# Another order of the same instructions: priorities disturbed from a recorded list of 82 seeds in place of the best of 105 candidates

## The chip, the cores and the metric

The kernel runs on one core of a Trainium2 chip. A core has TensorE (PE, with its weight loads shown apart as PEld), VectorE (DVE), ScalarE (ACT), GpSimd (POOL) and SyncE (SP), which here issues every DMA. The metric is the device time of one execution in microseconds; the kernel is given by the median of its runs.

## The reference

x is 2048 tokens of 512 features. The result is x + s * g. s is a linear attention block on the normalised x with 32 heads of 16 features, g is the silu of a gated feed-forward block on the raw x with 1792 hidden features:

```python
def _A_ref(x, wqkv, wo):                       # H = 32, Dh = 16
    ...
    phi = lambda t: jnp.where(t > 0, t + 1, jnp.exp(t)) + 1e-6
    pq, pk = phi(q), phi(k)
    kv = jnp.einsum("bhsd,bhse->bhde", pk, v)
    z = jnp.einsum("bhsd->bhd", pk)
    num = jnp.einsum("bhqd,bhde->bhqe", pq, kv)
    den = jnp.einsum("bhqd,bhd->bhq", pq, z)[..., None] + 1e-6
    o = num / den
    return (...) @ wo

def _B_ref(x, w_gate, w_up, w_down):
    return (_gelu(x @ w_gate) * (x @ w_up)) @ w_down

x = A_x
xn = _layernorm(x, axis=-1)
s = _A_ref(xn, A_wqkv, A_wo)
g = _silu(_B_ref(xn, B_w_gate, B_w_up, B_w_down))
return x + s * g
```

## The kernel before, in words

Each large matrix product is done by a scheme with seven block products in place of eight (numbered 1 to 7 in the code), and each factor is split into a high and a low part (names that end in h and l), so that a product is three matmuls per block of 128 rows, a group of six for two blocks. One 512-column matmul is the unit of work on PE.

The program has four stages. In the first, x is loaded tile by tile, normalised and transposed (tiles x, xn, pt), its transposed forms Xh and Xl are made, keys and queries are computed (X, Y, Z, k, q) and the products of keys and x are summed up in four banks (gps). The queries and the forms of x for the first half go out to DRAM. In the second and third stage the feed-forward block is computed for the second half of the tokens and then for the first: quads of products FX, FY, FZ for one block of the gate or up weights, whose result h is split into seven forms hf0 to hf6 with a high and a low part, and down products DX, DY, DZ, which VectorE adds to acc. In the second stage the weights are taken from the inputs, brought into their forms and kept in DRAM (w_d, wd_d); the third stage loads them from there (w<-w_d, wd<-wd_d) and, between its quads, fetches the queries (q<-q_d), divides them (GpSimd makes u, VectorE den and q) and transposes them (ptq). Between these stages stand the small products of the attention block (pkv, pm), and the forms of x for the first half are loaded back (Xh<-xh_d, Xl<-xl_d). The last stage multiplies the queries with the folded attention weights (SX, SY, SZ), multiplies the result with the silu of the feed-forward block (g, acc), transposes it (rt), adds x (xp) and stores it (out_y).

No instruction is issued while the stages are described. Each call of do() only notes an operation: its engine, its planned duration (for example pool(n) is 0.15 + 0.00214 * n us), its dependences, and for a DMA its size. At the end Plan.order() makes one list of all operations, and they are issued in that list's order; every engine runs its own in the order of the list and waits on semaphores. So the list fixes each engine's queue, SP's DMA issues included.

Plan.run() is a list scheduler: an engine that is free takes, of the operations that are ready, the one with the lowest value in late. With the argument chain it also keeps to the stated order of the PE operations, pe_keys; with wide it does not. link() sets the lag between dependent operations, with three margins: to PE, to the other engines, and on the landing of a DMA. Plan.replay() goes through a finished list with the planned durations and gives start times and a total. A run backwards (with self.behind) turns start times into new values of late.

Before, order() did this for three sets of margins with 35 rounds each, noted for every round the total of a replay without margins, and gave back the list with the lowest one; where the best of a set of margins had not improved for more than two rounds, late was disturbed at random for all operations at once:

```python
if best is None or true < best[0] - 1e-6:
    best = true, done, at
...
if same > 2:
    size = rng.choice((0.05, 0.2, 0.5))
    late = [t + rng.uniform(-size, size) for t in late]
```

Of the kernel before, what the change touches and what calls it, by code (L numbers as in the profile page):

```python
# [75 lines left out]
class Plan:  # L76
# [6 lines left out]
    SLOW, FULL = 1.3, 6.0  # L83
    WAY = 0.45
    BEGIN = 0.65
    ROUNDS = 35
    MARGINS = ((0.1, 0.18, 1.0), (0.2, 0.06, 1.0), (0.1, 0.12, 1.0))
    SEED = 2
    WAIT = 0.3
    FIXED = 4  # L90

# [96 lines left out]
    def run(self, nxt, late):  # L188
# [75 lines left out]
        return start, done  # L264

    def replay(self, order):

        info = self.info
        ready, start = [self.BEGIN] * len(order), [0.0] * len(order)
        left = [len(row) for row in self.behind]  # L270
        queue = {e: collections.deque() for e in self.TAIL}
# [5 lines left out]
        while n < len(order):  # L277
            turn = None
            for e, q in queue.items():
                if q and not left[q[0]]:  # L280
                    t = max(free[e], ready[q[0]])
                    t = (max(t, port) if info[q[0]][2] else t, t, e)
                    if turn is None or t < turn:
                        turn = t
            when, _, eng = turn
            pick = queue[eng].popleft()
            n += 1
            _, cost, lock, move = info[pick]
            start[pick] = when
            end = free[eng] = when + cost  # L290
            if lock:
                port = end
            if eng == "SP":
                dma = max(dma, end + self.WAY)
                dma += move * (self.SLOW if dma < self.FULL else 1.0)
                end = dma
            last = max(last, end)
            for j, lag in self.ahead[pick]:
                if end + lag > ready[j]:
                    ready[j] = end + lag  # L300
                left[j] -= 1
        return last, start

    def order(self, pe_keys):
        self.link(pe_keys, 0.0, 0.0, 0.0)
        plain = self.ahead
        best, rng = None, random.Random(self.SEED)
        for margins in self.MARGINS:
            chain = self.link(pe_keys, *margins)
            wide = self.ahead  # L310
            late = self.tails(chain)
            low = min(late)
            late = [t - low for t in late]
            top, same = None, 0
            for n in range(self.ROUNDS):
                start, done = self.run(chain if n < self.FIXED else wide, late)
                total, real = self.replay(done)
                self.ahead = plain
                true, at = self.replay(done)
                self.ahead = wide  # L320
                if best is None or true < best[0] - 1e-6:
                    best = true, done, at
                if top is None or true < top[0] - 1e-6:
                    top = true, total, done, real
                    same = 0
                same += 1
                if same > 2:
                    _, total, done, real = top
                back = self.behind
                if n < self.FIXED - 1:  # L330
                    back = [[] for _ in chain]
                    for i, row in enumerate(chain):
                        for j, lag in row:
                            back[j].append((i, lag))
                start, _ = self.run(back, [total - t - c[1] for t, c in zip(real, self.info)])
                late = [total - t - c[1] for t, c in zip(start, self.info)]
                if same > 2:
                    size = rng.choice((0.05, 0.2, 0.5))
                    late = [t + rng.uniform(-size, size) for t in late]
            self.log(best[0])  # L340
        self.at = {self.ops[i]: t for i, t in enumerate(best[2])}
        return [self.ops[i] for i in best[1]]

    def log(self, total):
        pass
# [1077 lines left out]
```

## Time and profile before

| | |
|---|---|
| median of 3 runs | 612.13 us (610.62, 612.13, 614.85) |
| profiled execution, its own time | 610.86 us |
| its span, first to last instruction | 609.1 us |
| instructions | 8384 |
| PE busy | 601.8 us, 2754 matmuls |
| VectorE, GpSimd, ScalarE busy | 479.7, 359.9, 336.2 us |
| DMA | 143.16 MB, 67.2% of 16 engines' span in the main queue |

All rows come from one profiled execution, whose time lies between the lowest run and the median. The span leaves out what lies before the first and after the last instruction of the program, 1.7 us. A busy share says how long an engine had an instruction in work; matmuls overlap, since one is shown from its start to its modelled end and the next begins before that.

### The profile page before, as it was taken

Reading aid. Unit: us, or ns where it says so; the run is one execution under the profiler, and the core shown is the slowest. Engines: PE = TensorE matmul, PEld = TensorE weight load, DVE = VectorE, ACT = ScalarE, POOL = GpSimd, SP = SyncE. Lnnn points to the kernel's source line nnn. Section 1 sums busy time; section 2 is a strip of 40 time slices with the busy share of each in tenths; the row PEclk is TensorE's granted clock in tenths of the full one; section 3 lists DMA queues with packets and bytes.
Section 4 is the critical chain, followed back from the end, with each engine's and each line's share of the span. In section 5 each row is a group of like instructions: output and inputs, shape, how many; then the busy total and the mean of one; then the engine's idle time right before and its main releaser. Section 6 shows DMA issues by size and latency. Waiting matters only on the chain.

```text
span 609.1 us, 8384 instructions
## 1 busy us (share of the span) xinstructions
PE 601.8 (99%) x2754; PEld 496.2 (81%) x2754; DVE 479.7 (79%) x712; ACT 336.2 (55%) x610; POOL 359.9 (59%) x300
## 2 busy tenths in 40 slices
PE   9999999999999999999999999999999999999996
PEld 8888888888888888888888788888888888878884
DVE  6999988785887998788878556677837875879886
ACT  6787778785676635653564154545224522677520
POOL 5834644544879768967785047267306641686970
PEclk9999999999999999999999999999999999999999
DMA  7369521249768648864669799898558855996346
GB/s 241 101 217 305 190 69 71 86 156 343 278 210 291 225 151 312 314 210 170 210 241 404 297 350 414 317 290 270 159 204 273 291 168 189 331 337 217 119 162 218
DMA packets 69659, 143.16 MB, mean 235 GB/s; under 512 B 5616, under 2 KB 28144, under 8 KB 69616
## 3 DMA queue, kind: packets, MB, share of 16 engines
q1 hardware_dynamic: 69616, 142.63, 67.2%
q8 instruction: 22, 0.36, 0.3%
q14 instruction: 21, 0.17, 0.1%
HBM read 81.00 MB, written 61.60 MB: 234 GB/s over the span
## 4 chain that ended last, share of the span: by engine, by line
PE 96%; DVE 1%; DMA 1%; POOL 0%; issue 0%; ACT 0%; DVEq 0%
PE FX L496 24%; PE DX L496 13%; PE FZ L496 12%; PE gps L496 7%; PE DZ L496 6%; PE FY L496 6%; PE X L496 5%; PE SX L496 4%; PE DY L496 3%; PE Z L496 3%; PE k L496 2%; PE SZ L496 2%; PE q L496 2%; PE Y L496 1%; PE pt L666 1%; PE ptq L1148 1%
## 5 line engine op out<-in xcount | busy, mean ns | idle before, releaser
L496 PE MATMUL FX<-Xh,w 128*128 128x512 f32 x448 | 152.5, 390 | 0.0
L1056 POOL TENSOR_TENSOR h<-h,g 128x512 f32<-128x512 f32 x42 | 62.9, 1500 | 96.4 <-DVE h L480 95.0
L496 PEld LDWEIGHTS FX<-Xh,w 128*128 128x128 f32 x448 | 83.8, 188 | 17.2
L480 POOL TENSOR_TENSOR h<-h,h 128x512 f32<-128x512 f32 x56 | 84.5, 1508 | 12.9 <-DVE hf6l L480 4.1
L496 PE MATMUL FX<-Xl,w 128*128 128x512 f32 x224 | 87.4, 390 | 0.0
L496 PE MATMUL FZ<-Xh,w 128*128 128x512 f32 x224 | 78.5, 391 | 0.0
L474 ACT COPY fu<-FX 128x512 f32<-128x512 f32 x56 | 32.9, 587 | 66.9 <-PE FX L496 65.0
L496 PE MATMUL gps<-pks,xns 128*128 128x512 f32 x192 | 51.0, 391 | 0.0
L496 PEld LDWEIGHTS FX<-Xl,w 128*128 128x128 f32 x224 | 42.1, 188 | 8.7
L496 PEld LDWEIGHTS FZ<-Xh,w 128*128 128x128 f32 x224 | 41.7, 188 | 9.0 <-DVE g L480 0.6
L742 POOL TENSOR_TENSOR zacc<-zacc,kp 128x512 f32<-128x512 f32 x16 | 24.2, 1511 | 37.0 <-DVE kp L731 31.0
L496 PE MATMUL FZ<-Xl,w 128*128 128x512 f32 x112 | 43.9, 392 | 0.0
L1082 DVE TENSOR_TENSOR acc<-acc,DX 128x512 f32<-128x512 f32 x48 | 32.6, 682 | 14.3 <-PE DX L496 13.9
L496 PEld LDWEIGHTS gps<-pks,xns 128*128 128x128 f32 x192 | 35.9, 188 | 7.4
L496 PE MATMUL FY<-Xh,w 128*128 128x512 f32 x112 | 39.5, 394 | 0.0
L480 DVE TENSOR_TENSOR g<-fu,FZ 128x512 f32<-128x512 f32 x28 | 19.2, 685 | 17.0 <-PE FZ L496 7.7
L1082 DVE TENSOR_TENSOR acc<-acc,DZ 128x512 f32<-128x512 f32 x32 | 21.9, 683 | 12.7 <-PE DZ L496 9.0
L496 PE MATMUL X<-kq,Xh 128*128 128x512 f32 x96 | 31.1, 397 | 0.0
L1048 ACT ACTIVATE g<-g 128x512 f32<-128x512 f32 x42 | 26.6, 632 | 7.9 <-DVE g L480 7.8
L480 DVE TENSOR_TENSOR h<-fu,FZ 128x512 f32<-128x512 f32 x28 | 19.2, 685 | 14.3 <-PE FZ L496 7.6
L480 POOL TENSOR_TENSOR u<-q,zacc 128x512 f32<-128x512 f32 x16 | 21.0, 1331 | 11.9 <-DMA q<-q_d 11.3
L496 PEld LDWEIGHTS FY<-Xh,w 128*128 128x128 f32 x112 | 21.0, 188 | 4.7 <-issue 0.5
(413 smaller groups left out, 1621.3 us busy)
## 6 DMA issues: line engine op xcount, KB each, us to landing
w_d<-w SPq DMA_DIRECT2D x36, 512.0 KB, 5.1
w<-w_d SPq DMA_DIRECT2D x36, 512.0 KB, 5.1
wd_d<-wd SPq DMA_DIRECT2D x21, 512.0 KB, 4.9
wd<-wd_d SPq DMA_DIRECT2D x21, 512.0 KB, 5.6
x<-in_A_x SPq DMA_DIRECT2D x16, 256.0 KB, 4.0
q_d<-qp SPq DMA_DIRECT2D x16, 256.0 KB, 2.2
q<-q_d SPq DMA_DIRECT2D x16, 256.0 KB, 5.2
pn_d<-pT SPq DMA_DIRECT2D x8, 512.0 KB, 6.4
```

Source lines behind the costliest of these rows:

```text
L474: do("ACT", act(n), lambda o, i: nc.scalar.copy(o, i), dst, src, name=name)
L480: do(eng, c, lambda o, p, q: getattr(e, f"tensor_{op}")(o, p, q), dst, a, b, name=name)
L496: nc.tensor.matmul(o, v[i], v[i + 1], start=start and part == 0 and i == 0, stop=stop and part == 1 and i == len(v) - 2, skip_group_check=on)
L666: nc.tensor.transpose(o[:, k, :], a[:, k * P:(k + 1) * P], b)
L742: do("POOL", pool(D), lambda o, i: nc.gpsimd.tensor_add(o, o, i), zacc, p0, name="zacc")
L1048: curved("gelu", do("ACT", curve(NC), lambda o, i: nc.scalar.activation(o, i, AF.Gelu_apprx_tanh), g, ps if e is None else g, name="gelu"))
L1056: do("POOL", pool(NC), lambda o, i: nc.gpsimd.tensor_mul(o, o, i), h, g, name="h")
L1082: do("DVE", dve(NC), lambda o, i: nc.vector.tensor_add(o, o, i), a, ps, name="acc")
L1148: nc.tensor.transpose(o[:, k, :], a[:, k * P:(k + 1) * P], b)
```

## The change

The operations, their planned durations and their dependences stay as they are. order() first makes one list: 14 rounds with the margins (0.1, 0.12, 1.0), the first four with the stated order of PE and the others without, no random part, no comparison of rounds. Then it goes through a list of 82 seeds. For each, nudged() draws an instant of the plan, a width of 4, 10 or 25 us before it, a size of 0.2, 0.6 or 2.0 us and a share of 0.1, 0.4 or 1.0, and adds a random amount of up to that size to late for that share of the operations which the last plan started between that width before the instant and 2 us after it. Plan.run() then schedules all operations anew. The disturbed priorities are kept from seed to seed, and the list after the last seed is the one issued. The search that picked the seeds (by the mean of eight replays with longer operations and landings) is not part of the kernel.

```diff
@@ -83,9 +83,9 @@
     SLOW, FULL = 1.3, 6.0
     WAY = 0.45
     BEGIN = 0.65
-    ROUNDS = 35
-    MARGINS = ((0.1, 0.18, 1.0), (0.2, 0.06, 1.0), (0.1, 0.12, 1.0))
-    SEED = 2
+    ROUNDS = 14
+    MARGIN = (0.1, 0.12, 1.0)
+    STEPS = (4, 5, 15, 18, 44, 51, 56, 57, 89, 96, 99, 103, ...)
     WAIT = 0.3
     FIXED = 4
 
@@ -301,45 +301,55 @@
                 left[j] -= 1
         return last, start
 
+    def plan_times(self, done):
+
+        keep, self.ahead = self.ahead, self.plain
+        _, at = self.replay(done)
+        self.ahead = keep
+        return at
+
+    def first_order(self, pe_keys):
+
+        self.link(pe_keys, 0.0, 0.0, 0.0)
+        self.plain = self.ahead
+        chain = self.link(pe_keys, *self.MARGIN)
+        self.wide = self.ahead
+        late = self.tails(chain)
+        low = min(late)
+        late = [t - low for t in late]
+        for n in range(self.ROUNDS):
+            _, done = self.run(chain if n < self.FIXED else self.wide, late)
+            if n == self.ROUNDS - 1:
+                break
+            total, real = self.replay(done)
+            back = self.behind
+            if n < self.FIXED - 1:
+                back = [[] for _ in chain]
+                for i, row in enumerate(chain):
+                    for j, lag in row:
+                        back[j].append((i, lag))
+            start, _ = self.run(back, [total - t - c[1] for t, c in zip(real, self.info)])
+            late = [total - t - c[1] for t, c in zip(start, self.info)]
+        return late, done
+
+    def nudged(self, late, at, seed):
+
+        rng = random.Random(seed)
+        t = rng.uniform(0.0, max(at))
+        width, size, share = rng.choice((4.0, 10.0, 25.0)), rng.choice((0.2, 0.6, 2.0)), rng.choice((0.1, 0.4, 1.0))
+        return [v + rng.uniform(-size, size) if t - width < a < t + 2.0 and rng.random() < share else v for v, a in zip(late, at)]
+
     def order(self, pe_keys):
-        self.link(pe_keys, 0.0, 0.0, 0.0)
-        plain = self.ahead
-        best, rng = None, random.Random(self.SEED)
-        for margins in self.MARGINS:
-            chain = self.link(pe_keys, *margins)
-            wide = self.ahead
-            late = self.tails(chain)
-            low = min(late)
-            late = [t - low for t in late]
-            top, same = None, 0
-            for n in range(self.ROUNDS):
-                start, done = self.run(chain if n < self.FIXED else wide, late)
-                total, real = self.replay(done)
-                self.ahead = plain
-                true, at = self.replay(done)
-                self.ahead = wide
-                if best is None or true < best[0] - 1e-6:
-                    best = true, done, at
-                if top is None or true < top[0] - 1e-6:
-                    top = true, total, done, real
-                    same = 0
-                same += 1
-                if same > 2:
-                    _, total, done, real = top
-                back = self.behind
-                if n < self.FIXED - 1:
-                    back = [[] for _ in chain]
-                    for i, row in enumerate(chain):
-                        for j, lag in row:
-                            back[j].append((i, lag))
-                start, _ = self.run(back, [total - t - c[1] for t, c in zip(real, self.info)])
-                late = [total - t - c[1] for t, c in zip(start, self.info)]
-                if same > 2:
-                    size = rng.choice((0.05, 0.2, 0.5))
-                    late = [t + rng.uniform(-size, size) for t in late]
-            self.log(best[0])
-        self.at = {self.ops[i]: t for i, t in enumerate(best[2])}
-        return [self.ops[i] for i in best[1]]
+
+        late, done = self.first_order(pe_keys)
+        at = self.plan_times(done)
+        for seed in self.STEPS:
+            late = self.nudged(late, at, seed)
+            _, done = self.run(self.wide, late)
+            at = self.plan_times(done)
+        self.at = {self.ops[i]: t for i, t in enumerate(at)}
+        self.log(max(at))
+        return [self.ops[i] for i in done]
 
     def log(self, total):
         pass
```

The list STEPS is cut here; it has 82 numbers from 4 to 6222.

## Rows read from the trace of the kernel before

**Rows 1.** The page: span, and busy us (share) x instructions per engine

```profile
span 609.1 us, 8384 instructions
...
PE 601.8 (99%) x2754; PEld 496.2 (81%) x2754; DVE 479.7 (79%) x712; ACT 336.2 (55%) x610; POOL 359.9 (59%) x300
```

**Rows 2.** Chain that ended last, in order of time: start us, us, what

```profile
143.11 1.36 PE FX L496 x6
...
151.72 1.58 PE FZ L496 x6
...
545.91 1.61 PE DX L496 x6
```

**Rows 3.** PE's waits: engine line waited for: us in total, times, longest us

```profile
PE warm L518 <- DVE ones L507: 1.2, 1, 1.2
PE rt L1350 <- DVE acc L1329: 0.7, 1, 0.7
PE ptq L1148 <- DVE q L1142: 0.2, 1, 0.2
```

**Rows 4.** Waits of the weight loads (PEld), same columns

```profile
PEld warm L518 <- DVE ones L507: 1.1, 1, 1.1
PEld rt L1350 <- DVE acc L1329: 0.9, 1, 0.9
PEld DX L496 <- issue: 0.7, 3, 0.2
PEld ptq L1148 <- DVE q L1142: 0.7, 1, 0.7
PEld FZ L496 <- DVE g L480: 0.6, 2, 0.3
PEld rt L1350 <- PE SX L496: 0.5, 1, 0.5
PEld pm L1247 <- issue: 0.5, 2, 0.2
PEld FY L496 <- issue: 0.5, 2, 0.2
...
PEld DX L496 <- ACT hf0h L474: 0.4, 1, 0.4
...
PEld Y L496 <- DVE qp L731: 0.2, 1, 0.2
```

**Rows 5.** The chain's end, and PE's last instruction in the timeline

```profile
601.99 0.70 DVE su L480
...
602.71 0.69 DVE acc L1329
...
603.46 0.65 PE L1350 MATMUL rt<-ident,acc 128*128 128x128 f32 x4 [0.70 <-DVE acc L1329]
```

**Rows 6.** GpSimd's costliest group; VectorE's hf0l: ns min/median/max

```profile
L1056 POOL TENSOR_TENSOR h<-h,g 128x512 f32<-128x512 f32 x42 | 62.9, 1500 | 96.4 <-DVE h L480 95.0 <-ACT w L474 1.3
...
L480 DVE TENSOR_TENSOR hf0l<-h,hf0h x14: 675/1024/1794, 156.0 to 551.2; 128x512 fp32r<-128x512 f32 x14
```

**Rows 7.** Loads of weights w<-w_d, from issue to landing

```profile
DMA to landing us min/median/max: 3.2/5.1/9.0
```

**Rows 8.** Windows: PE, PEld, DVE, ACT, POOL busy (x), clock, DMA share, GB/s

```profile
360.00:370.00 10.00, 10.00 (x46) 8.28 (x45) 4.64 (x7) 4.52 (x9) 2.58 (x2) 1.00 1.03 408
...
600.00:605.00 5.00, 3.41 (x21) 2.54 (x19) 4.54 (x12) 0.00 (x0) 0.00 (x0) 1.00 0.43 119
605.00:609.20 4.20, 0.00 (x0) 0.00 (x0) 0.39 (x2) 0.00 (x0) 0.00 (x0) 0.82 0.59 166
```

**Rows 9.** The chain around the queries' return, in order of time

```profile
399.91 5.38 DMA q<-q_d
...
412.84 0.66 PE ptq L1148 x4
```

More of the change, by code (lines that the diff above doesn't have):

```diff
@@ L85 @@
     BEGIN = 0.65
-    ROUNDS = 35
-    MARGINS = ((0.1, 0.18, 1.0), (0.2, 0.06, 1.0), (0.1, 0.12, 1.0))
-    SEED = 2
+    ROUNDS = 14
+    MARGIN = (0.1, 0.12, 1.0)
+    STEPS = (4, 5, 15, 18, 44, 51, 56, 57, 89, 96, 99, 103, 108, 109, 130, 138, 141, 183, 201, 238, 268, 271, 282, 373, 377, 396, 416, 424, 428, 482, 493, 498, 595, 625, 642, 672, 676, 732, 742, 762, 792, 796, 841, 1040, 1047, 1149, 1221, 1230, 1387, 1598, 1892, 1900, 1959, 2078, 2132, 2281, 2447, 2600, 2633, 2713, 2735, 2834, 3177, 3308, 3441, 3485, 4328, 4412, 4416, 4443, 5266, 5279, 5349, 5701, 5724, 5787, 6022, 6088, 6130, 6163, 6188, 6222)
     WAIT = 0.3
```

## Prediction

> **What bounds the kernel now.** I read the totals first: TensorE (PE) is busy for 601.8 of 609.1 us [rows 1]. A share like that can still hide stalls, because a matmul's end is modelled. So I next read the chain that ended last, in order of time: a chain piece of six 512-column matmuls takes 1.36 us, that is 0.227 us from start to start, and most pieces of the chain are of exactly that length [rows 2]. The same rows show what a stall looks like: the piece of six at 151.72 us took 1.58 us, 0.22 more, the one at 545.91 us took 1.61, 0.25 more [rows 2]. The third view is who waited for whom. PE itself has only three waits, 1.2 us at the very start, 0.7 and 0.2 us [rows 3]. The loading of weights (PEld) runs a step ahead of PE, so it shows the same waits longer, and more of them: eighteen groups [rows 4]. The reader should see there that there is no large wait left: after the start the longest single one is 0.9 us. No DMA is a releaser in either list.
>
> So the bound is the number of matmuls times 0.227 us, plus a start of 1.15 us, plus an end. PE's last instruction ends at 603.46 + 0.65 = 604.11 us (603.46 is the transposition that waits for the last multiply) and the span ends at 609.1: some 5.0 us in which VectorE adds the last transposed block and the last stores land [rows 5]. Large idle times of ScalarE or GpSimd cost nothing here.
>
> **The change part by part.**
>
> *Work.* The program's operations, their sizes and dependences are untouched. Instructions removed: none, added: none. The 2754 matmuls cost the same 0.227 us each (or their narrower price), so the work term is 0.
>
> *What moves.* The old code took, of 105 candidate orders, the one that was shortest in a replay with the planned durations. The new code makes 14 rounds with one set of margins, and then 82 local disturbances of the priorities; each is followed by a new list scheduling, and the last order is used whatever its own replay says. Any operation can therefore change its place in the queue of PE, ScalarE, VectorE, GpSimd or SP, the DMA issues too. The diff does not say which do: this cannot be followed move by move before it is built, so I bound it by the places where PE loses time now.
>
> *What a better order can give back inside.* The eighteen PEld groups sum to 1.1 + 0.9 + 0.7 + 0.7 + 0.6 + 0.5 + 0.5 + 0.5 + 0.4 + 0.4 + 0.4 + 0.3 + 0.3 + five times 0.2 = 8.3 us [rows 4]; thirteen of the groups, from 0.7 for the transposition of q to 0.2 for Y, are waits for another engine's result that an order can remove. The start (1.1) and the last transposition (0.9) stay in any order. Three groups put down to issue (0.7 + 0.5 + 0.5) sit around the four two-pass multiplications called pm and go with these wherever they stand. That leaves 8.3 - 1.1 - 0.9 - 1.7 = 4.6 us, in fifteen waits. PE loses less than PEld waits, as PEld is ahead: at 545.91 us PEld waited 0.40 (the group for hf0h, 0.4) and PE lost 0.25. With that 0.15 less for each, 4.6 - 15 x 0.15 = 2.4 us; with the 0.08 of the other pair (0.30 of the 0.6 for two waits on g, against 0.22) it is 3.4. I take 2.8 us as what PE loses to order inside, an estimate between these two. Lower end of the gain: 0 (the same number of such handovers remains), upper end: 3.4.
>
> *What the end can give.* In the old order the last product is an SZ, and its result passes an addition (su, 0.70 us at 601.99) and a multiplication (0.69) before the last transposition [rows 5]. The product numbered 4 ends in a multiplication alone. Were it the last one, 0.70 us would go. Nothing in the diff favours it, so I enter 0, with 0.7 as the bound.
>
> *What a new order costs.* Every order meets the chip with handovers that the plan did not foresee. GpSimd's 512-column operation is charged 0.15 + 0.00214 x 512 = 1.25 us in the plan and takes 1.50 us on the chip [rows 6], and VectorE's subtraction hf0l, 0.68 at its quickest, has a median of 1.02 and took up to 1.79 us [rows 6]. When such an operation is the one PE needs next, the excess is paid by PE: between 0 and 1.79 - 0.68 = 1.11 us, and nearest to the waits that exist, which are 0.2 to 0.4 us [rows 4]. The new search lowered a mean over replays with longer operations and landings, so such handovers should be rarer, not gone: two of 0.25 us, the size at 545.91, cost 0.5 us.
>
> The Trainium skill's page SBUF — State Buffer, section "Who interferes with whom", has it that a VectorE operation with two SBUF inputs and a GpSimd operation exclude each other at a shared port for a whole instruction. The spread of hf0l, 0.68 to 1.79 us, agrees. By that rule alone one new handover would cost up to a whole GpSimd operation, 1.50 us, in place of the 0.5, and the sum would come out 1.0 us higher.
>
> *DMA landings.* A load of weights (512 KB) lands in 5.1 us at the median, 9.0 at most [rows 7], and from 320 to 390 us the 16 DMA engines are full, share 1.03 in the row shown [rows 8]. In the old order PE never waited for one directly; the nearest is the chain by which a query block comes back (5.38 us of landing from 399.91), passes GpSimd and VectorE and is transposed at 412.84, where PEld had waited 0.7 us [rows 9, 4]. What hides the loads is the PE work queued between issue and use. If this cover were gone for one load, the price is 9.0 - 5.1 = 3.9 us. The lower bound is 0, and a gain is excluded, as no load is on PE's path alone. I take 0 and keep 3.9 for the range.
>
> *The sum.* Half of the 2.8 us goes: -1.4. New handovers: +0.5. End: 0. Work: 0. The profiled execution took 610.86 us, 1.7 us more than its span; it becomes 610.86 - 1.4 + 0.5 = 609.96. The three runs shown have a median of 612.13, 1.27 above the profiled execution, with one at 614.85. I do not know what those runs lost; if it is late landings, an order chosen under longer landings should lose less, and I keep half of the 1.27: 609.96 + 0.64 = 610.6 us.
>
> **The rivals.**
>
> *It changes nothing that can be seen.* The new waits are as many as the old ones: -2.8 + 2.8, and the median stays at 612.1. For it: PE starts its matmuls without a gap almost everywhere already, and the places that stall are handovers at which little other work is ready. Against it: fifteen separate waits are just what moving single operations can mend.
>
> *A load comes late, and the kernel is slower.* Place: the reload of the transformed x and the first weights of the second pass, from 320 to 390 us, where the DMA engines are full [rows 8]; mechanism: an issue that the new order puts one load later on SP lands behind its neighbour. One such miss costs 3.9 us, 610.86 + 3.9 = 614.8; two cost 7.8, 618.7. It decides from the point at which the spare time of a load is under 3.9 us. Against it: both orders are planned with the same 1.0 us of margin on landings, and the selection of the new one lengthened landings. For it: the new code does not compare its final order with the best nominal one.
>
> *The clock falls.* The granted clock is 1.00 from start to end while PE works, with no idle time of PE over 0.70 us after the start, and is lower only in the last 4.2 us, after PE's last instruction [rows 3, 8]. A hole long enough for the 1.2 GHz level would make each following matmul take about twice its 0.227 us until the clock is back: 20 of them are 4.5 us, on top of the hole of about 4 that a late load makes, so 610.86 + 8.4 = 619.3. The page TensorE: Matmul & The Clock Gate of the Trainium skill, section "HAM oscillation — how this bites in real kernels", says that waits of PE for a DMA throw the clock back to its lower level; no stretch inside this trace shows it. This needs the late load first.
>
> *All of it works.* Waits -3.4, end -0.7, no new handover, and the runs no longer scatter: 610.86 - 4.1 = 606.8. Only with the lowest of the three runs as a guide (0.24 below) does it touch 606.5. A gain above 1% (below 606.0) would need more than everything that I can find.
>
> **How the numbers follow.** About 1%, some 6 us, is what a measurement of this kernel can tell from no change. Chances: the small gain (607.5 to 611.4) 0.50; nothing seen (611.4 to 614) 0.33; one late load (614 to 618) 0.09; slower by more, two late loads or the clock, 0.05; everything works, below 607.5, 0.03. The likeliest is the small gain, and its time is 610.6. The range takes in the gain down to 607.5 and, with the old order's slowest run and one late load, up to 615; left out are 0.03 below and some 0.1 above. Of the 0.03 below, 0.02 lies under 606.0: faster 0.02, slower 0.05, plus 0.01 for what I have not thought of, 0.06; same 0.92.
>
> **What would show it.** PE busy near 600 to 602 us with the same 2754 matmuls, six of them in 1.36 us almost throughout. PEld's waits for other engines, 4.6 us now, should sum to 2 to 4; the one for q near 412 us and those for hf6l, hf0h and hf0l are the ones that I expect smaller. No DMA should stand as releaser of PE or PEld. The stretch after PE's last instruction should stay near 5.0 us. The prediction is wrong if PE or PEld waits for one DMA for several us, if the clock drops inside the span, or if the span falls under 605 us, which would say that time was lost in a way these views don't show.

## The result and the profile after

The changed order is slower: 614.47 us median against 612.21 for the kernel before (20 runs each), a ratio of 1.0033 with a 95% interval of 1.0020 to 1.0045. That is under the 1% that I called telling, but clear of zero, and on the other side of my forecast of a small gain.

The profiled execution of the changed kernel took 615.96 us, 1.5 above its median; that of the kernel before took 610.86, 1.35 below its own. So the two traces, 613.8 and 609.1 us of span, differ by 4.7 us, about twice what the medians do. They show where time is lost, and the sizes have to come from the comparisons of many runs.

The page of the changed kernel, the rows that answer to [rows 1]:

```profile
span 613.8 us, 8378 instructions
...
PE 603.1 (98%) x2754; PEld 497.5 (81%) x2754; DVE 474.4 (77%) x712; ACT 335.8 (55%) x610; POOL 354.3 (58%) x300
```

The same 2754 matmuls keep PE busy 603.1 us instead of 601.8, so most of the 4.7 us is PE standing still. Counted in the order of their starts, the matmuls of the two traces have the same forms in each of four stretches, so these can be compared: up to the 121st matmul the changed kernel takes 0.96 us more, from there to the 2401st 0.51 less, from there to the 2601st 3.50 more, and from there to the end of the span 0.70 more. Who PE waited for, all rows of the view (engine, line, us in total, times, longest), which answer to [rows 3]:

```profile
PE DX L506 <- ACT hf0h L484: 2.0, 1, 2.0
PE rt L1360 <- DVE xp L1366: 1.4, 2, 1.1
PE warm L528 <- DVE ones L517: 1.1, 1, 1.1
PE k L506 <- ACT Xh L484: 1.0, 1, 1.0
PE rt L1360 <- DVE acc L1339: 0.6, 1, 0.6
```

Before there were three waits, 1.2, 0.7 and 0.2 us. Three are new, and they are the three places of this study: the start (k, 1.0), the handover from the feed-forward block to the last stage (hf0h, 2.0), and the end (rt, 1.4). The wait for q is gone from the list.

*The handover.* ScalarE from 540 to 550 us in the timeline (start us, us, engine line op, in brackets the idle time before and what ended it):

```profile
544.14 0.62 ACT L484 CAST hf0h<-h 128x512 fp32r<-128x512 f32 x1 [0.90 <-POOL h L490]
546.94 0.63 ACT L1125 ACTIVATE g<-g 128x512 f32<-128x512 f32 x1 [2.18 <-DMA g<-g_d]
547.48 0.60 ACT L484 CAST hf0h<-h 128x512 fp32r<-128x512 f32 x1
547.99 0.63 ACT L1125 ACTIVATE g<-g 128x512 f32<-128x512 f32 x1
```

ScalarE takes its instructions in order. At 544.8 us the next one is the silu of g, a reloaded result of the other half of the tokens that only the last stage's multiplications need; its data is on the way and lands at 546.9. Behind it waits the cast hf0h, and behind the cast waits PE. The cast's input was not what was missing: in the run below that has no silu in its way (e3) it starts at 545.72. The load itself is late because of SP's queue. SP before, and then SP after:

```profile
536.85 0.32 SPq L449 DMA_DIRECT2D g<-g_d  x1
537.90 0.80 SPq L449 DMA_DIRECT2D pb<-pn_d  x2
538.79 0.38 SPq L449 DMA_DIRECT2D ms<-m_d  x1
539.22 1.12 SPq L449 DMA_DIRECT2D g<-g_d  x2
```

```profile
535.29 1.91 SPq L459 DMA_DIRECT2D ms<-m_d  x2
539.24 0.80 SPq L459 DMA_DIRECT2D pb<-pn_d  x2
540.12 0.38 SPq L459 DMA_DIRECT2D ms<-m_d  x1
540.60 0.86 SPq L459 DMA_DIRECT2D g<-g_d  x2
```

The second g was issued ahead of two loads pb and one of ms; now it stands behind them, 3.75 us later. SP is in order too: the loads pb read back what the store pn_d<-pT has written, and SP stood still until that store had landed, with the g now behind it. Its waits from 530 to 545 us, before and after:

```profile
SPq L449 <- DMA pn_d<-pT: 0.7, 1, 0.7
```

```profile
SPq L459 <- DMA pn_d<-pT: 2.0, 1, 2.0
```

The pattern on ScalarE is not new, only its size. Before, the silu of the third g stood directly ahead of this same cast:

```profile
545.36 0.63 ACT L1115 ACTIVATE g<-g 128x512 f32<-128x512 f32 x1 [1.41 <-DMA g<-g_d]
545.90 0.60 ACT L474 CAST hf0h<-h 128x512 fp32r<-128x512 f32 x1
```

That g was issued at 539.22, and PE lost 0.25 us [rows 2]. The g that the cast now stands behind is issued at 540.60, 1.4 us later, and PE comes to that place 0.4 us sooner. PE in the same stretch after the change:

```profile
545.53 0.61 PE L506 MATMUL DX<-hf1h,wd 128*128 128x512 f32 x2
548.13 0.50 PE L506 MATMUL DX<-hf0h,wd 128*128 128x512 f32 x1 [1.99 <-ACT hf0h L484]
...
549.44 0.63 PE L506 MATMUL DX<-hf1l,wd 128*128 128x512 f32 x1
549.87 0.63 PE L506 MATMUL DX<-hf1h,wd 128*128 128x512 f32 x1
```

After the hole, from 549.44 on, eight matmuls start 0.43 us apart in place of 0.227. The windows of 5 us (columns as in [rows 8]) say why: the clock column, 1.00 before and after, shows

```profile
545.00:550.00 5.00, 3.01 (x13) 2.11 (x12) 3.55 (x5) 2.53 (x5) 4.84 (x4) 0.94 1.02 387
550.00:555.00 5.00, 5.00 (x18) 3.95 (x17) 3.19 (x6) 4.10 (x8) 2.76 (x3) 0.72 0.55 183
```

which is a stretch at the 1.2 GHz level. Note that PE is shown busy for the full 5.00 us of the second window; only the count (18 matmuls instead of 24) and the clock tell. The price is 8 x 0.20 = 1.6 us on top of the hole.

*The end.* PE's last instructions in the timeline, which answer to [rows 5]:

```profile
605.81 0.63 PE L1360 MATMUL rt<-ident,acc 128*128 128x128 f32 x4 [0.26 <-DVE xp L1366]
607.05 0.66 PE L1360 MATMUL rt<-ident,acc 128*128 128x128 f32 x4 [0.61 <-DVE acc L1339]
608.79 0.63 PE L1360 MATMUL rt<-ident,acc 128*128 128x128 f32 x4 [1.09 <-DVE xp L1366]
```

There is now one more transposition after the one that waits for the last multiplication. It needs no late data, but a PSUM bank, and that bank is read by two adds to xp, of which VectorE has the second behind three others.

*The start.* ScalarE in the timeline:

```profile
7.93 0.37 ACT L484 CAST Xh<-pt 128x256 fp32r<-128x256 f32 x1
8.35 0.62 ACT L484 CAST kq<-wk 128x512 fp32r<-128x512 f32 x1
8.87 0.36 ACT L484 CAST Xh<-pt 128x256 fp32r<-128x256 f32 x1
```

Between the two casts Xh that the first product k needs, there now stands a cast of a weight, which waits for the landing of wk at 8.32 us (read off the chain). It is the handover's pattern again. Before, both casts Xh came first.

*The middle.* From 40 to 520 us PEld waited for other engines 0.7 + 0.4 + 0.3 + 0.2 + 0.2 = 1.8 us before; after, the largest rows of the same view and window are

```profile
PEld pt L676 <- PE X L506: 0.5, 1, 0.5
PEld ptq L1158 <- DVE q L1152: 0.5, 2, 0.3
...
PEld pm L1257 <- PE DX L506: 0.2, 1, 0.2
```

and with three more of 0.2 (FX twice, pm) they sum to 1.8 us as well. But 0.7 of this is put down to PE itself; for other engines it is 1.1. That fits the 0.51 us that the stretch from the 121st to the 2401st matmul is shorter.

### The profile page after: what moved, and what is told of

Its sections match the earlier page's. It is cut to its first block, busy times and chain, and to the rows that moved or that the text cites. A ratio compares the mean times of both kernels' runs of the same rounds, so it can differ in the third digit from the quotient of the medians.

```text
span 613.8 us, 8378 instructions
## 1 busy us (share of the span) xinstructions
PE 603.1 (98%) x2754; PEld 497.5 (81%) x2754; DVE 474.4 (77%) x712; ACT 335.8 (55%) x610; POOL 354.3 (58%) x300
## 4 chain that ended last, share of the span: by engine, by line
PE 94%; DMA 3%; DVE 1%; ACT 1%; POOL 0%; SPq 0%; issue 0%; DVEq 0%; POOLq 0%; ACTq 0%
PE FX L506 24%; PE FZ L506 12%; PE DX L506 12%; PE gps L506 7%; PE FY L506 6%; PE DZ L506 6%; PE X L506 5%; PE SX L506 3%; PE Z L506 3%; PE DY L506 3%; PE k L506 2%; PE q L506 2%; PE SZ L506 2%; PE Y L506 1%; PE ptq L1158 1%; PE pt L676 1%
## 5 line engine op out<-in xcount | busy, mean ns | idle before, releaser
L484 ACT COPY fe<-FX 128x512 f32<-128x512 f32 x28 | 16.4, 586 | 17.8 <-PE FX L506 15.4
```

Of the source, the lines that this page charges most:

```text
L484: do("ACT", act(n), lambda o, i: nc.scalar.copy(o, i), dst, src, name=name)
```

## The experiments

Theory Q, for queue: the list puts, into an engine's strict queue, an instruction that waits for a DMA ahead of one that PE needs soon, and PE pays. Its rivals were S, scatter (the holes are accidents of one execution and the loss is many small waits), and in single runs L, H and E, named there. All kernels issue the same operations; only positions in the list differ. Two tools were used: a splice, which takes the operations of a stretch of the plan's time from one list and the others from the other list, and a move of single operations, here by their number: 2890 is the load of the second g, 2896, 2899 and 2900 are the silus of the second to fourth g, 2743 and 2748 the last two casts hf0h, 22 the cast of wk, 65 the second cast Xh, 3098 and 3100 the two adds to xp that free the bank. In a move (a, b, 0) a goes directly ahead of b, in (a, b, 1) directly behind it. Each ratio is to the kernel before, run beside it.

**e1_mid_before: a splice that cut at a bad seam.**

```diff
+    PIECES = ((520.0, "after"), (560.0, "before"), (1e9, "after"))
```

> The changed order, but the operations between 520 and 560 us of the plan stand in the order of the kernel before. In the profile of the change PE stood still for 2.0 us at 546 us, waiting for ScalarE's cast hf0h, and the granted clock then fell, so that eight matmuls began 0.43 us apart in place of 0.227. Theory Q (queue): the hole comes from the order of this stretch, so both go. The hole is 2.15 us against 0.43 lost there before, the eight matmuls 8 x 0.2 = 1.6, together 3.3 us: 614.5 - 3.3 = 611.2, a ratio to the kernel before of 0.998, granted clock 0.999, no wait of PE over 0.5 us between 540 and 560 us. Theory S (scatter): the hole is an accident of the one profiled execution and the median is slower through many small waits; then the ratio stays at 1.003.

Measured: 617.08 us, 1.0074 (1.0052 to 1.0095): slower than either order, which neither theory had. The hole at 546 us shrank to 0.3 us, but the seam at 520 made another one. Its PE rows in the timeline:

```profile
525.27 0.90 PE L566 MATMUL FX<-Xh,w 128*128 128x512 f32 x2 [2.07 <-ACT fu L544]
525.97 0.63 PE L566 MATMUL FX<-Xl,w 128*128 128x512 f32 x1
526.39 0.63 PE L566 MATMUL FX<-Xh,w 128*128 128x512 f32 x1
```

and ScalarE's:

```profile
524.11 0.62 ACT L544 CAST hf1h<-h 128x512 fp32r<-128x512 f32 x1 [2.75 <-POOL h L550]
524.64 0.58 ACT L544 COPY fu<-FX 128x512 f32<-128x512 f32 x1
```

A cast that waits for GpSimd stands ahead of the copy fu that PE waits for; in the changed order the copy came first, at 522.19. Again eight matmuls follow 0.43 us apart. As a test of the handover the run is void; its trace shows the same pattern in ScalarE's queue without a DMA, behind a wait for GpSimd.

**e2_mid_after: the stretch alone, put into the kernel before.**

```diff
+    PIECES = ((520.0, "before"), (560.0, "after"), (1e9, "before"))
```

> The kernel before, with only the operations between 520 and 560 us of the plan in the changed order. Theory Q: the hole comes with them, 612.2 + 3.3 = 615.5, a ratio of 1.005, granted clock 0.995 to 0.997, PE waiting for hf0h about 2 us. Theory S: 612.2, a ratio of 1.000.

Measured: 613.76 us, 1.0018 (1.0006 to 1.0031). The hole came with the stretch:

```profile
PE DX L566 <- ACT hf0h L544: 1.3, 1, 1.3
```

but smaller, and after it the clock column stays at 1.00. So the direction is Q's, the size about a third of the 3.3 us that I had read off one trace.

**e3_silu_later: three silus moved on ScalarE.**

```diff
+    MOVES = ((2896, 2748, 1), (2899, 2896, 1), (2900, 2899, 1))
```

> The changed order with three instructions moved on ScalarE alone: the silus of the second, third and fourth reloaded g, which wait for a landing, stand behind the last cast hf0h in place of before and between the last two. In the profile of the change the first of them waited 2.18 us for its load and the cast behind it is what PE waited for. Theory Q: the hole closes and the clock stays, 614.5 - 3.3 = 611.2 or a ratio of 0.998, although the load is as late as before. Rival L: PE is held by something else in that stretch (GpSimd's subtractions that make the cast's input, which ended only a little earlier), so the cast starts hardly sooner and the ratio stays at 1.002 to 1.003.

Measured: 612.7 us, 1.0008 (0.9992 to 1.0023), 0.25% below the changed order. In its trace the casts follow GpSimd without the load between them, and PE has no wait in that stretch:

```profile
545.72 0.62 ACT L544 CAST hf0h<-h 128x512 fp32r<-128x512 f32 x1 [0.74 <-POOL h L550]
547.41 0.62 ACT L544 CAST hf0h<-h 128x512 fp32r<-128x512 f32 x1 [1.07 <-POOL h L550]
547.94 1.15 ACT L1185 ACTIVATE g<-g 128x512 f32<-128x512 f32 x2
```

Rival L falls. The gain is smaller than 3.3 us, as in e2.

**e4_load_sooner: one DMA issue moved on SP.**

```diff
+    MOVES = ((2890, 2863, 0),)
```

> The changed order with one DMA issue moved on SP alone: the load of the second g stands ahead of two loads of query blocks and one of weights, as in the kernel before, in place of behind them (it was issued at 540.6 us, before at 536.9). ScalarE's order is left as it is. Theory Q: the silu finds its data, the hole closes wholly or to the 0.4 us of before: 611.2 to 612, a ratio of 0.998 to 1.000. If the next load's landing or GpSimd is as late, the hole shrinks by less than half: 1.002.

Measured: 612.32 us, 0.9994 (0.9981 to 1.0006), 0.39% below the changed order. This one instruction takes back all that the median lost. Its trace has no wait of PE for hf0h; PEld's are 0.5 and 0.3 us. Both halves of Q are shown: without the late issue the queue's order does no harm, and without the queue's order the late issue does hardly any (e3).

**e5_head_one: one cast moved on ScalarE at the start.**

```diff
+    MOVES = ((22, 65, 1),)
```

> The changed order with one instruction moved on ScalarE: the third cast kq of the start, which waits for the landing of wk (8.32 us in the profile of the change), stands behind the second cast Xh in place of before it. PE's first product k waited 1.0 us for that Xh (0.2 before the change). Theory Q (a queue that waits for a landing ahead of what PE needs): k begins up to 0.9 us sooner, 614.5 - 0.9 = 613.6, a ratio to the kernel before of 1.002. Rival H: the start is set by the landings of x and wk themselves, and what k gains is lost again at the next transposition, which waited about 1 us for xn in three of the four runs just seen, with either order of the start: the ratio stays at 1.003.

Measured: 613.98 us, 1.0024 (1.0007 to 1.0041), between the two predictions and not to be told from either by its time. The traces of all runs say more. PE's waits for Xh (before k) and for xn (before the next transposition) together were, in five kernels that start as the changed one, 1.0, 1.1 (e1), 2.9 (e3), 1.7 (e4) and 2.5 us (e6), mean 1.8; with the cast moved 0.9, 0.8 (e7), 1.1 (e11) and 1.0 (e12), mean 0.95; in five kernels that start as the one before 0, 1.0 (e2), 0 (e8), 0.8 (e9) and 0 (e10), mean 0.4. So the start of the changed order loses more and scatters more, and the cast is part of it; the rest, the order of the first loads on SP, was not tried alone.

**e6_tail_one: one add moved on VectorE at the end.**

```diff
+    MOVES = ((3100, 3098, 1),)
```

> The changed order with one instruction moved on VectorE: of the adds to xp at the end, the second one that reads the first of the last four transposed blocks stands directly behind the first one, in place of three adds later. The last transposition goes into the bank that these two adds read, and waited 1.1 us for it in the profile of the change (there was no such wait before the change). Theory: the last transposition starts 1.1 us sooner, VectorE's remaining adds then set the end, and 0.8 to 1.2 us go, 614.5 - 1.0 = 613.5, a ratio of 1.0015. Rival E: the stores, issued one after the other on SP, set the end, and less than 0.3 us goes: 1.003.

Measured: 614.03 us, 1.0021 (1.0001 to 1.0040), by its time again not to be told from the changed order. The wait is gone, though, the last two transpositions being one row now:

```profile
605.42 1.38 PE L1420 MATMUL rt<-ident,acc 128*128 128x128 f32 x8 [0.60 <-DVE acc L1399]
```

VectorE is then done 608.02 - 605.42 = 2.6 us after the start of that row, where the changed order had 610.21 - 607.05 = 3.2. But from there to the end of the span it is 612.2 - 605.4 = 6.8 us against 613.8 - 607.05 = 6.7: nothing gained. SP's queue shows why. The stores out_y that SP issues after the last multiplication, in the changed order, in this run, and before the change (start us, us in all, count):

```profile
607.35 4.09 SPq L459 DMA_DIRECT2D out_y<-xp  x8
```

```profile
605.73 4.09 SPq L519 DMA_DIRECT2D out_y<-xp  x8
```

```profile
603.76 3.03 SPq L449 DMA_DIRECT2D out_y<-xp  x6
```

Eight stores back to back, 0.53 us apart, take 4.09 us whatever VectorE does; before there were six. That is rival E, and e12 tests it. The traces of all kernels here agree: from the transposition behind the last multiplication to the end of the span it is 5.7 to 5.8 us in the six with six stores, and 6.7 to 6.9 in seven of the eight with eight (8.0 in e4, whose last store landed later), while VectorE's end behind that transposition lies anywhere between 2.6 and 3.6 us in these eight.

**e7_three_moves: e4, e5 and e6 together.**

```diff
+    MOVES = ((2890, 2863, 0), (3100, 3098, 1), (22, 65, 1))
```

> The changed order with three instructions moved: the load of g of e4_load_sooner, the cast of e5_head_one, the add of e6_tail_one. If the three places are all that the change lost, their gains add up: 612.3 (e4_load_sooner) - 1.0 - 0 to 0.9 = 610.4 to 611.3, a ratio of 0.996 to 0.998, and the rest of the changed order is worth 1 to 2 us against the kernel before. If they don't add, because the time goes to the next late thing: 1.000.

Measured: 612.66 us, 1.0000 (0.9984 to 1.0017). Three moved instructions make the changed order as fast as the one before. They don't add to more than that, and not to more than e4 alone.

**e8_rest_after: the middle of the changed order.**

```diff
+    PIECES = ((40.0, "before"), (575.0, "after"), (1e9, "before"))
+    MOVES = ((2890, 2863, 0),)
```

> The changed order from 40 to 575 us of the plan, with the load of g moved as in e4_load_sooner, between the start and the end of the kernel before. It asks what the 530 us in the middle of the changed order are worth. The step of the prediction under test: fewer small waits there, a gain of about 1.4 us less 0.5, so 611.3, a ratio of 0.9985. Rival: what the profile shows there is 1 us less in one execution and scatter otherwise; 612.2 to 612.7, a ratio of 1.000.

Measured: 612.68 us, 1.0007 (0.9990 to 1.0025). The 530 us in the middle are worth nothing that can be measured, and the gain of 0.9 us that the prediction had there (0.9985) lies just outside the interval. The seam at 575 cost a wait of PE of 0.7 us for sf1l in its trace, so a gain of half a microsecond, as in the two traces above, is not ruled out.

**e9_two_into_before: two instructions put into the kernel before.**

```diff
+    PIECES = ((1e9, "before"),)
+    MOVES = ((2890, 2839, 1), (2896, 2743, 0))
```

> The kernel before with two instructions moved as the change has them: on SP the load of the second g behind two loads of query blocks and one of weights, on ScalarE its silu from four places earlier to directly ahead of the last cast but one, hf0h, that PE needs. Theory Q: these two alone make the hole; PE waits 1 to 2.2 us for hf0h near 546 us, 612.5 + 1 to 3 = 613.5 to 615.5, a ratio of 1.002 to 1.005. Rival: the hole needs the rest of the changed order too (GpSimd and the other loads of that stretch), then PE waits at most 0.5 us there and the ratio is 1.000.

Measured: 613.91 us, 1.0017 (0.9999 to 1.0034), not clear of 1 by a hair. Its trace has a hole, 0.9 us of PE behind

```profile
549.31 1.15 ACT L1185 ACTIVATE g<-g 128x512 f32<-128x512 f32 x2 [2.08 <-DMA g<-g_d]
```

but not quite the changed order's. The first of these two silus is the third g's, which this list, like that of the kernel before, has ahead of the cast (in the changed order it is behind it). Its landing ended the wait: in the chain that ended last, 6.12 us from its issue at 543.11. Set against the last DX ahead of the hole (545.97 us before, 549.46 here), it landed 0.4 us later than before, as the second g is now issued directly ahead of it, and the moved silu adds 0.5 us; PE's next matmul comes 1.0 us later than before. So the two moves lengthen the old wait; that they alone make the hole of the changed order is not shown.

**e10_before_silu_later and e11_five_moves: can either order be bettered?**

```diff
+    PIECES = ((1e9, "before"),)
+    MOVES = ((2896, 2748, 1), (2899, 2896, 1), (2900, 2899, 1))
```

> The kernel before with the same three silus moved behind the last cast hf0h as in e3_silu_later. PE lost 0.4 us there before the change, in two waits. Theory Q: these go, and with them what late landings cost in some executions: 612.5 - 0.4 to 1.0 = 611.5 to 612.1, a ratio of 0.998 to 0.9995. Rival: the silus are needed by then on ScalarE's own path, and their delay shows up in the last stage: 1.001.

```diff
+    MOVES = ((2890, 2863, 0), (3100, 3098, 1), (22, 65, 1), (2896, 2748, 1), (2899, 2896, 1),
+             (2900, 2899, 1), (3064, 3092, 0), (3066, 3064, 1))
```

> The changed order with the moves of e7_three_moves, the silus of e3_silu_later as well, and on VectorE two more adds to xp put ahead of a multiplication, as PE's second last transposition but one waited 0.3 us for their bank. Expected if small waits at fixed places add up: e7_three_moves (1.000) less 0.3 to 0.7 us, a ratio of 0.999. Rival: what is left in either order is the scatter of the landings at the start, and nothing is gained: 1.000 to 1.001.

Measured: 612.25 us, 0.9995 (0.9980 to 1.0010), and 611.99 us, 0.9989 (0.9977 to 1.0001). Both intervals hold 1, so neither is shown to beat the kernel before; e11, with eight instructions moved, is clearly faster than the changed order that it starts from (1.0033).

**e12_end_sooner: six stores at the end in place of eight.** 3097 is the transposition whose data was ready early, 3098 and 3100 are its adds, 3099 and 3101 their stores, 3059 an add that frees its bank.

```diff
+    MOVES = ((2890, 2863, 0), (22, 65, 1), (2896, 2748, 1), (2899, 2896, 1), (2900, 2899, 1),
+             (3059, 3061, 1), (3097, 3090, 0), (3098, 3089, 1), (3100, 3098, 1), (3099, 3060, 1), (3101, 3099, 1))
```

> What sets the end, and can the changed order be mended to beat both? In the changed order's trace SP issues eight stores one after the other after the last multiplication, 0.53 us apart, from 607.35 to 611.44; in the trace of the kernel before six, from 603.76 to 606.79. In e6_tail_one VectorE was done 0.6 us sooner after that multiplication, and the eight stores ended as late as before. Two of the eight belong to a transposition whose data was ready long before. This kernel is the changed order with the load of g, the casts and the silus of e11_five_moves, and with that transposition ahead of the last two products, its two adds and stores with it. Theory: the stores on SP set the end, six are left, 2 x 0.53 = 1.1 us go from the stretch between the last multiplication and the end (6.7 us to 5.7), and the kernel is at 0.9989 - 0.0017 = 0.997 of the kernel before. Rival: VectorE's adds set the end or PE loses the time at the earlier transposition, the stretch is shorter by less than 0.4 us, and the ratio stays at 0.999.

Measured: 611.18 us, 0.9980 (0.9964 to 0.9995): faster than either order, by 0.2% and 0.5%. In its trace

```profile
602.19 0.63 PE L1420 MATMUL rt<-ident,acc 128*128 128x128 f32 x4 [0.68 <-DVE xp L1426]
603.42 1.09 PE L1420 MATMUL rt<-ident,acc 128*128 128x128 f32 x8 [0.60 <-DVE acc L1399]
```

the stretch from the transposition behind the last multiplication to the end of the span is 609.1 - 603.4 = 5.7 us, as the theory said and as before the change (609.1 - 603.46). With e6, where VectorE alone was sooner and nothing went, the rival for the end falls: the stores on SP set it. Against e11 the time alone does not show it (0.9980 and 0.9989). The ratio came out one tenth of a per cent above the forecast; the first row, a wait for a bank that the changed order has as 0.26 us, cost 0.4 of the 1.1 us.

## Why the prediction was wrong

*What bounds the kernel.* Right. The same matmuls at 0.227 us, and little else; all that was lost was lost by PE standing still, or at the lower clock.

*The gain inside (-1.4).* Too large. I took half of what PE loses to handovers as mendable. The new order mended some (the wait for q) and made others: between the 121st and the 2401st matmul it is 0.51 us shorter in the two traces, and e8 can't tell the middle from 0. Also, of the 4.6 us of PEld's waits that I put down to other engines, 0.7 name PE itself (0.5 of it at rt [rows 4]).

*The cost of new handovers (+0.5).* This is the step that failed. I sized them by the waits that the old order had, 0.2 to 0.4 us, and took two. But the old order's waits are what its search had left over. A new order's waits are as large as the thing that an in-order engine can be made to stand behind, here a landing: PE's wait for hf0h was 2.0, 1.2 (e5) and 0.7 us (e6) in the changed order where it was not mended, and 1.3 where its stretch was put into the kernel before (e2). It is the main loss: e4 takes back 0.39%, e3 0.25%, of the 0.33%.

*The start (left as it is).* Wrong too: I held that the start stays in any order. PE's waits for Xh and xn were 1.4 us longer there, 1.8 against 0.4 on the mean, and 0.9 of this went where the cast was moved (e5, e7, e11, e12).

*DMA landings (0, with 3.9 as the bound).* The mechanism of my second rival, an issue that the new order puts later on SP, is what happened. I had looked for it where PE needs the load itself, in the stretch where the DMA engines are full, and wrote that no DMA releases PE. That is true of the changed kernel's trace as well: the DMA releases ScalarE, and PE sees only ScalarE. (In the traces of e2, e4, e6, e8 and e9 PE does wait for loads, 0.2 to 1.0 us ahead of pkv, with either order in that place.) The row to look at was the old order's own: ScalarE waited 1.41 us for the third g before, and PEld had its 0.4 us for hf0h right behind it.

*The clock.* The rival came with a hole of about 4 us, and priced 20 matmuls. Here the clock fell after a hole of 2.0 us, and eight matmuls paid, 1.6 us; that it falls inside the span was one of my signs of being wrong. The Trainium skill, TensorE: Matmul & The Clock Gate, section "HAM oscillation — how this bites in real kernels", has PE's waits for a DMA throwing the clock back; in the changed kernel's trace and in e1's it fell after waits as well, of 2.0 and 2.1 us, though for ScalarE.

*The end (0).* Wrong by about 1 us, and by a thing that I had not priced: how many stores stand in SP's queue after the last multiplication. I had read the 5.0 us behind PE's last instruction as fixed, an add and a landing. It is the stores, 0.53 us each, and the new order left two more for the end (6.7 us from the transposition behind the last multiplication, against 5.7). The new wait of 1.1 us for a bank, which looks like the cause in PE's list, hid behind them (e6).

*The median.* I kept half of the distance between the profiled execution and the median, on the ground that an order chosen under longer landings loses less to them. The runs give no sign of that: they scatter from 612.74 to 617.31 us, those of the kernel before from 610.62 to 614.85. The start is one place where the changed order scatters more (1.0 to 2.9 us without the moved cast).

Why the search took such an order is argued, not shown. The plan charges a load of 256 KB that finds no other in its way 0.475 + 0.45 + 256/365 + 1.3 = 2.9 us from issue to landing, plus 1.0 of margin while it schedules; with the loads in its way, the kernel's replay has the second g land 4.5 us after its issue and 1.2 us ahead of its silu. In the changed trace the loads of g between 530 and 552 us took

```profile
DMA to landing us min/median/max: 3.3/5.4/7.5
```

and this one 6.3, 1.7 us more than planned, so an order that looks safe by 1.2 us is late by 0.5; the rest of the hole I put down to the late issue. Replays with longer landings can only help if they are longer by that much; how long they were is not in the kernel.

Open: how much of the 0.33% is the hole, the start and the end each. The three single moves measured 0.39, 0.09 and 0.12% below the changed order, each uncertain by some 0.2%, and together (e7) 0.33%, so their times don't tell them apart further. The traces, one of each kernel, say a little more. From the 2401st to the 2601st matmul it is 45.4 to 45.7 us in the kernel before and in all runs without the hole (e3, e4, e7, e8, e10, e11, e12), and 49.1, 46.7 and 46.1 in the changed order, e5 and e6, 1.8 us more on the mean. The start takes 1.4 us more where the cast is not moved, the stretch from the 2601st matmul on 0.8 more with eight stores, and the middle 0.8 less (these two by their medians). That is 3.2 us in all against 2.3 between the medians, and it makes e4, which keeps the start and the end, 1.4 us slower than the kernel before, which its median doesn't show: part of its 0.39% is probably luck.

## What to carry to other kernels

In an order that a planner makes, look through every in-order queue for an instruction that waits for a landing and is not urgent, with one behind it that the bound engine needs; the profile shows it as idle time of that engine ended by a DMA, one row ahead of the wait of the bound engine. Moving one such instruction took back, by the medians, all that a whole search had lost. At the end, count the stores that are issued after the last result: they run one behind the other. A new order has to be judged by the largest wait that its queues allow, not by the waits that the old one happened to have.

## What the runs showed of the hardware

After a wait of PE of 2.0 us (the changed order) and one of 2.1 us (e1_mid_before), the granted clock went to its lower level although PE had been busy for hundreds of us before, and eight matmuls started 0.43 us apart before it came back. After waits of 1.3 (e2) and 1.2 us (e5) in the same place no such stretch followed. A hole on PE thus had a second price here, of nearly its own size.

Stores of 128 KB that SP issued one behind the other started 0.53 us apart, and the end of the kernel followed their number: eight took 4.09 us to issue, six 3.03. A load that stood behind SP's wait for the landing of a store was issued late with it (2.0 us of SP standing still in the changed order).
